# A pair's value product moved behind the next turn's scores, and scale totals moved to another PSUM bank, in attention followed by two gated MLPs

## The chip, the cores and the metric

The kernel runs on one core of a Trainium2 chip. The metric is device time in microseconds (us) from start to end of the program, as a median over runs. TensorE multiplies matrices into PSUM, ScalarE (ACT) and VectorE (DVE) read PSUM and compute element by element, GpSimd (POOL) does little here, and SyncE (SP) issues nearly all DMAs from one queue, in order.

## The reference

```python
def _attn_ref(q, k, v, g_q, g_k):          # 4 batches, 12 heads, 448 rows, 64 columns
    q_n, k_n = (rmsnorm(q, g_q), rmsnorm(k, g_k))
    scores = scale * np.matmul(q_n, k_n.transpose(0, 1, 3, 2))
    scores = scores - np.max(scores, axis=-1, keepdims=True)
    attn = np.exp(scores)
    attn = attn / (np.sum(attn, axis=-1, keepdims=True) + 1e-09)
    return np.matmul(attn, v)

def _moe_ref(x, w_a, w_b, w_out):          # x: 1792 x 768, hidden 1536
    return (x @ w_a) * (x @ w_b) @ w_out

def _moe2_ref(x, w_in, w_out, alpha):      # hidden 2048
    h = x @ w_in
    g = np.maximum(h, 0.0) + alpha * np.minimum(h, 0.0)
    return g @ w_out
```

The attention's output, all heads side by side, is the input of the first MLP, whose output is the input of the second. The weights come as 64-bit floats.

## The kernel before, in words

**Products.** Each of the four batches goes through four stages: `a` (24 products, w_a and w_b alternating, multiplied into `ab`), `y` (6), `h` (16) and `o` (6). They are named a0, y0, h0, o0, a1 and so on, and run in the order of the list `stages`. A number is held as two halves of 16 bits, so a product takes three matmuls for each block of 128 x 128: 18 matmuls for a product of `a` and `h`, 36 for one of `y`, 48 for one of `o`. A product accumulates in one of three PSUM banks (tiles `p`, pool `ps_m`). It is read out by L779 (ACT) and L782 (DVE) in `a`, L820 (ACT) in `y`, L857 and L858 in `h`, L876 (ACT) in `o`.

**Scales.** Halves of 16 bits need a scale by a power of two. For a stage's results it comes from the sum of their squares: L785 (in `a`, ACT) or L821 (in `y`) squares, a matmul with ones adds up over the partitions, VectorE makes the power, and then L760 (ACT) and L761 (DVE) split the results. So at the end of a stage all its results must be there before the next stage that uses them can start. Weights are converted on their first use, in a0, y0, h0 and o0 (L644, L647, L650, L658, then L705 and L706 behind a total over their squares), and kept in DRAM for the later batches, from where they are loaded four products ahead. All totals over squares go through `total` (tile `tot`), whose bank `x` (pool `ps_x`, one buffer) also serves the value products (tile `x`) and the norm of `y` (tile `norm`).

**Attention.** Heads go in pairs, six to a batch, 24 in all. `att_steps` is a generator. Its turn `m` issues the scores of step m + 1 (two chunks of 64 rows for two heads; seven chunks make a pair, so a pair takes three and a half turns), the softmax of step m (`soft`: maximum L417 on DVE, L430 and two exponentials L434 on ACT), the probabilities of step m - 1 (`probs`: L479 on ACT and L480 on DVE write one of four buffers `p16`, which a transposing DMA, L486, brings into `pT`), some preparation of later pairs (squares L232, L235, casts L341, L343), and, when a pair's chunks are all there, its value product `pv` (24 matmuls; 8 in batch 0, which uses 32-bit numbers) and `pv_out` (L530 on ACT, L531 on DVE), which reads it out of bank `x`. `pT` has one buffer: the next pair's transposes wait until the value product has read it. A turn has three yields.

**What runs when.** Ahead of a0 the loop `while done < NP` runs whole turns until the six pairs of batch 0 are done. From there each stage draws as many yields as the table `RATE` gives it, spread over its products, so that batches 1 to 3 are computed between products up to y2; a3 and the later stages have no attention. A scheduler then orders each engine's instructions, by the order in which they were written and by when it thinks that they can run; what it has made is fixed in the program.

Of the kernel before, what the change touches and what calls it, by code (L numbers as in the profile page):

```python
# [19 lines left out]
def attention_gated_mlps_kernel(  # L20
# [20 lines left out]
    NP = H // 2  # L41
# [79 lines left out]

    def total(cols, n, groups=1):

        ps = ps_x.tile([128, 512], F32, tag="x", name="tot")
        p = cols.shape[0]
        mm(ps[:, 0:n], ones[:p], cols, True, True)
        if n == groups:
            return ps[:, 0:n]
        t = sm_p.tile([128, 4], F32, tag="tot", name="tots")[:, 0:groups]
        nc.vector.reduce_sum(  # L130
            out=t, in_=ps[:, 0:n].rearrange("p (g k) -> p g k", g=groups), axis=AX.X
        )
        return t
# [406 lines left out]
    def att_steps():  # L540
        total = B * NP * NI // 2
        done = 0
        scores(0)
        for m in range(total + 3):
            if m + 1 < total:
                scores(m + 1)
            if m < total:
                soft(m)
            yield None
            if 1 <= m <= total:  # L550
                for _ in probs(m - 1):
                    yield None
            else:
                yield None
            fin = None
            for n in range(2 * m + 2 if m else 0, 2 * m + 4):
                g, c = divmod(n, NI)
                if n < 2 * total:
                    if g >= NP:
                        if c == 0 and g % NP == 0:  # L560
                            vscale(g // NP)
                        if c == 5:
                            vprep2(g)
                        if c == 6:
                            load_v(g + 2)
                    ahead = (g + 1, g + 2) if g % 2 else ()
                    if g > 1 and g % 2 == 0 and c == 6:
                        prep0(g + 2)
                    if c == 0:
                        for x in ahead[1 if g > 1 else 0:]:  # L570
                            prep0(x)
                    if c == 1 and ahead and g + 1 < B * NP:
                        prep1(ahead)
                    if g == 0 and c < NP:
                        vnorm(0, c)
                    if g == 1 and c == 0:
                        vscale(0)
                    if g == 0 and c < 3:
                        (prep3f, prep2f, prep4f)[c](1)
                    if 0 < g and g + 1 < B * NP and 2 <= c < 5:  # L580
                        (preps_f if g + 1 < NP else preps)[c - 2](g + 1)
                    if c == 5:
                        load_qk(g + 3)
                    if c == (6 if g % 2 or g < NP else 1) and g + NP < B * NP:
                        vnorm(g // NP + 1, g % NP)
            if done < B * NP and 2 * (m - 1) >= (done + 1) * NI:
                pv(done)
                pv_out(done)
                fin = done
                done += 1  # L590
            yield fin


    stages = "a0 y0 h0 o0 a1 y1 a2 h1 o1 y2 a3 h2 y3 o2 h3 o3".split()
# [323 lines left out]
    if True:  # L918
# [18 lines left out]
        n, done = 0, 0  # L937
        W0, EVERY = 4, 2
        while done < NP:
            g = [next(att) for _ in range(3)][-1]  # L940
            n += 1
            if n >= W0 and (n - W0) % EVERY == 0:
                advance((n - W0) // EVERY - 9 if n < 22 else -1)
            if n == 8:
                setup3()
                setup4()
            if g is not None:
                done += 1
# [51 lines left out]
```

## Time and profile before

| | |
|---|---|
| median of 3 runs | 1235.76 us (1233.34 to 1237.47) |
| profiled execution | 1237.6 us, span 1235.8 us |
| TensorE busy in the span | 1169.1 us (95%), 6574 matmuls |
| ScalarE busy | 738.8 us (60%) |
| VectorE busy | 677.4 us (55%) |
| mean granted TensorE clock | 0.981 |

The span is the time from the first to the last instruction. Busy shares are means over stages that differ: ScalarE and VectorE are busy nearly all the time early on, when weights are converted, and mostly idle at the end. Matmuls overlap, so that a busy TensorE isn't one at its peak; the time from one matmul's start to the next one's tells more. 1.0 of the granted clock is 2.4 GHz.

### The profile page before, as it was taken

How to read it: one execution, taken by the hardware profiler on the slowest of the kernel's cores; microseconds unless marked ns; L12 is line 12 of the kernel's file. 1: busy time of each engine (PE TensorE's matmuls, PEld its weight loads, DVE VectorE, ACT ScalarE, POOL GpSimd, SP SyncE). 2: the span in 40 equal slices, each digit the busy share in tenths (PEclk: the TensorE clock that was granted, in tenths of full speed). 3: DMA queues.
4: the chain of work that ended last, by engine and by line, in shares of the span. 5: the costliest groups of instructions: out<-in, count | busy, mean ns of one | idle time of the engine just before them, and what ended most of it. 6: DMA issues, size and time to landing. Idle time of an engine off the chain costs nothing.

```text
span 1235.8 us, 18195 instructions
## 1 busy us (share of the span) xinstructions
PE 1169.1 (95%) x6574; PEld 599.5 (49%) x6574; DVE 677.4 (55%) x1455; ACT 738.8 (60%) x1504; POOL 10.4 (1%) x32
## 2 busy tenths in 40 slices
PE   6997998989988999979999999999999999999998
PEld 4553554444534444435455454545555555554554
DVE  7898999889899667666551465331111440102400
ACT  7998999999889767676643465553221441213311
POOL 1000000000000000000000000000000000000000
PEclk9997999999999999989999999999999999999999
DMA  7558999999999999897854737876333333344343
GB/s 196 162 169 214 306 338 323 298 299 304 287 262 287 238 253 240 190 225 166 219 145 125 167 104 170 191 189 158 102 116 116 115 117 107 110 144 129 98 128 89
DMA packets 311243, 234.68 MB, mean 190 GB/s; under 512 B 175440, under 2 KB 284496, under 8 KB 311152
## 3 DMA queue, kind: packets, MB, share of 16 engines
q1 hardware_dynamic: 311040, 233.43, 71.7%
q8 instruction: 52, 0.85, 0.3%
q0 software_dynamic: 112, 0.07, 0.2%
q14 instruction: 39, 0.32, 0.1%
HBM read 155.79 MB, written 32.24 MB: 152 GB/s over the span
## 4 chain that ended last, share of the span: by engine, by line
PE 54%; DMA 2%; ACT 1%; DVE 1%; issue 0%; SPq 0%; ACTq 0%; DVEq 0%
PE p L107 49%; PE s L107 2%; PE x L107 2%; DMA pT<-p 2%; PE p L883 1%; ACT t L876 0%; PE norm L107 0%; ACT p L479 0%; ACT pf L434 0%; DVE nm L417 0%; SPq L486 0%; DVE ab L782 0%; DVE p L480 0%; DVE kr L332 0%; DVE qr L326 0%
## 5 line engine op out<-in xcount | busy, mean ns | idle before, releaser
L107 PEld LDWEIGHTS <-w 128*128 128x128 f16 x4896 | 476.7, 99 | 477.0 <-issue 49.7
L107 PE MATMUL p<-x,w 128*128 128x448 f16 x1728 | 336.8, 354 | 2.1 <-ACT t L779 2.0
L107 PE MATMUL p<-g,w 128*128 128x448 f16 x1152 | 229.5, 356 | 5.5 <-DVE g L844 2.1
L107 PE MATMUL p<-y,w 128*128 128x448 f16 x1152 | 224.7, 356 | 3.5 <-ACT y L760 3.2
L107 PE MATMUL p<-ab,w 128*128 128x448 f16 x864 | 170.8, 358 | 1.3 <-ACT ab L760 1.3
L417 DVE TENSOR_REDUCE nm<-s 128x2 f32<-128x896 f32 x84 | 91.1, 1085 | 41.7 <-PE s L107 41.3
L480 DVE SCALAR_TENSOR_TENSOR p<-pf,ri,p 128x448 f16<-128x448 f32 x126 | 84.4, 680 | 34.3 <-ACT p L479 34.0
L479 ACT ACTIVATE p<-pf,ri 128x448 f16<-128x448 f32 x126 | 81.4, 663 | 36.0 <-DMA pT<-p 28.1
L434 ACT ACTIVATE pf<-s,nm,esc 128x448 f32<-128x448 f32 x126 | 90.1, 719 | 1.3
L858 DVE SCALAR_TENSOR_TENSOR t<-t,al,p 128x448 f32<-128x448 f32 x55 | 37.3, 678 | 96.5 <-ACT t L857 96.5
L782 DVE SCALAR_TENSOR_TENSOR ab<-p,inv_a,t 128x448 f32<-128x448 f32 x48 | 32.5, 677 | 96.0 <-PE p L107 95.9
L706 DVE SCALAR_TENSOR_TENSOR w<-wf,sc,w 128x768 f16<-128x768 f32 (+1 forms) x76 | 70.2, 926 | 4.5 <-ACT w L705 4.1
L876 ACT ACTIVATE t<-p,inv_o 128x448 f32<-128x448 f32 x24 | 25.6, 1067 | 76.4 <-PE p L107 76.4
L785 ACT ACTIVATE junk<-ab 128x448 bf16<-128x448 f32 x48 | 27.4, 572 | 68.0 <-DVE ab L782 68.0
L650 DVE SCALAR_TENSOR_TENSOR wf<-raw,wf 128x768 int32<-128x768 int32 (+1 forms) x76 | 65.8, 867 | 0.5
L705 ACT ACTIVATE w<-wf,sc 128x768 f16<-128x768 f32 (+1 forms) x76 | 65.5, 866 | 0.0
L644 ACT ACTIVATE wf<-raw 128x768 f32<-128x768 f32 (+1 forms) x76 | 63.3, 838 | 1.6 <-DVE w L706 1.2
L658 ACT ACTIVATE junk<-wf 128x768 bf16<-128x768 f32 (+1 forms) x76 | 58.9, 775 | 2.9 <-DVE wf L650 2.5
L857 ACT ACTIVATE t<-p 128x448 f32<-128x448 f32 x55 | 29.7, 541 | 48.4 <-PE p L107 48.2
L843 ACT ACTIVATE g<-t,cgf 128x448 f16<-128x448 f32 x55 | 36.7, 668 | 34.6 <-DVE t L858 34.6
L107 PE MATMUL s<-kT,qT 128*64 128x448 f16 x252 | 50.2, 376 | 6.1 <-ACT pf L434 2.8
L844 DVE SCALAR_TENSOR_TENSOR g<-t,cgf,g 128x448 f16<-128x448 f32 x55 | 37.5, 682 | 29.6 <-ACT g L843 29.5
(140 smaller groups left out, 1065.1 us busy)
## 6 DMA issues: line engine op xcount, KB each, us to landing
w<-sc_a SPq DMA_DIRECT2D x72, 384.0 KB, 3.2
w<-sc_h SPq DMA_DIRECT2D x48, 384.0 KB, 3.0
w<-sc_o SPq DMA_DIRECT2D x72, 256.0 KB, 3.1
w<-sc_y SPq DMA_DIRECT2D x36, 384.0 KB, 3.2
raw<-in_moe_w_in_dram SPq DMA_DIRECT2D x16, 768.0 KB, 7.8
raw<-in_moe_w_out_dram SPq DMA_DIRECT2D x24, 512.0 KB, 5.9
raw<-in_moe_w_a_dram SPq DMA_DIRECT2D x12, 768.0 KB, 7.4
raw<-in_moe_w_b_dram SPq DMA_DIRECT2D x12, 768.0 KB, 7.5
```

What stands on the lines that cost most here:

```text
L107: nc.tensor.matmul(out=o, lhsT=a, rhs=b, start=first, stop=last)
L417: nc.vector.tensor_reduce(out=nm, in_=ps[:, :, 0:S], axis=AX.X, op=ALU.max, negate=True)
L434: nc.scalar.activation(out=pf, in_=ps[:, j, 0:S], func=AF.Exp, bias=nm[:, j:j + 1], scale=scale[j], accum_out=su[:, j:j + 1],)
L479: nc.scalar.activation(out=t[:, 0, :, 0:KP], in_=pf, func=AF.Copy, scale=r)
L480: nc.vector.scalar_tensor_tensor(out=t[:, 1, :, 0:KP], in0=pf, scalar=r, in1=t[:, 0, :, 0:KP], op0=ALU.mult, op1=ALU.subtract,)
L644: nc.scalar.activation(out=t, in_=hi.bitcast(F32), func=AF.Prelu, scale=2.0 ** -112, alpha=-(2.0 ** 32))
L650: nc.vector.scalar_tensor_tensor(out=ti, in0=lo, scalar=29, in1=ti, op0=ALU.logical_shift_right, op1=ALU.bitwise_or)
L658: nc.scalar.activation(out=junk(768, size(kind)), in_=t, func=AF.Square, accum_out=sums[0][:, j:j + 1])
L705: nc.scalar.activation(out=w[:, 0], in_=t, func=AF.Copy, scale=s)
L706: nc.vector.scalar_tensor_tensor(out=w[:, 1], in0=t, scalar=s, in1=w[:, 0], op0=ALU.mult, op1=ALU.subtract)
L844: nc.vector.scalar_tensor_tensor(out=x[:, 1], in0=t, scalar=cgf[:, f:f + 1], in1=x[:, 0], op0=ALU.mult, op1=ALU.subtract,)
L858: nc.vector.scalar_tensor_tensor(out=t, in0=t, scalar=al[:, f:f + 1], in1=ps, op0=ALU.mult, op1=ALU.add)
```

## The change

Two things change. The value product and its read-out (`pv`, `pv_out`) stand no longer at the end of turn m but right behind the scores at the start of turn m + 1, ahead of that turn's softmax. And `total` takes its bank from `new_ps`, which gives one of the three banks of the products, and no longer the bank `x`. The number of the finished pair comes with a turn's first yield, no longer with its third, and the loop ahead of a0 looks there.

```diff
     def total(cols, n, groups=1):
 
-        ps = ps_x.tile([128, 512], F32, tag="x", name="tot")
+        ps = new_ps()
         p = cols.shape[0]
...
         scores(0)
-        for m in range(total + 3):
+        for m in range(total + 4):
             if m + 1 < total:
                 scores(m + 1)
+            fin = None
+            if done < B * NP and 2 * (m - 2) >= (done + 1) * NI:
+                pv(done)
+                pv_out(done)
+                fin = done
+                done += 1
             if m < total:
                 soft(m)
-            yield None
+            yield fin
...
-            fin = None
             for n in range(2 * m + 2 if m else 0, 2 * m + 4):
...
-            if done < B * NP and 2 * (m - 1) >= (done + 1) * NI:
-                pv(done)
-                pv_out(done)
-                fin = done
-                done += 1
-            yield fin
+            yield None
...
         while done < NP:
-            g = [next(att) for _ in range(3)][-1]
+            g = [next(att) for _ in range(3)][0]
```

The scheduler makes a new order of all engines from this. The first place is ScalarE's queue just ahead of the read-out of pair 5's value product (L530), without which a0 can't finish a product. Before, in the built order:

```order
L644 ACTIVATE wf<-raw 128x768
L430 ACTIVATE nm<-nm,esc 128x2
L705 ACTIVATE w_1557<-wf,sc 128x768
L434 ACTIVATE pf,su<-s,nm,esc 128x448 x2
L462 COPY pT<-p 112x4x128 x2
L430 ACTIVATE nm<-nm,esc 128x2
L479 ACTIVATE p_2_110<-pf,ri 128x4x112
L434 ACTIVATE pf,su<-s,nm,esc 128x448 x2
L479 ACTIVATE p_3_111<-pf,ri 128x4x112
L658 ACTIVATE junk,ss<-wf 128x768
L530 ACTIVATE x_5_1467<-x,sx 128x448
```

The same place of ScalarE's queue with the change:

```order
L462 COPY pT<-p 112x4x128
L434 ACTIVATE pf,su<-s,nm,esc 128x448 x2
L462 COPY pT<-p 112x4x128
L430 ACTIVATE nm<-nm,esc 128x2
L235 ACTIVATE sq<-qr 128x448
L434 ACTIVATE pf,su<-s,nm,esc 128x448 x2
L479 ACTIVATE p_2_110<-pf,ri 128x4x112
L479 ACTIVATE p_3_111<-pf,ri 128x4x112
L430 ACTIVATE nm<-nm,esc 128x2
L232 ACTIVATE sk<-kr 112x512
L434 ACTIVATE pf,su<-s,nm,esc 128x448 x2
L530 ACTIVATE x_5_1476<-x,sx 128x448
```

A third softmax of 16-bit pairs stands ahead of L530, and squares of a later pair (L235, L232). Counted from the start of the queue, L434 stands 48 times ahead of this L530 instead of 46, L232 11 times instead of 9, L235 9 instead of 8, L430 3 instead of 2, and L644 9 instead of 10; the other lines as often as before.

The second place is ScalarE's queue at the end of y0, from the last squares (L821) to the first split for h0 (L760). Before:

```order
L821 ACTIVATE sq_2_2649<-y_0_5_3295 128x448
L434 ACTIVATE pf,su<-s,nm,esc 128x448 x2
L644 ACTIVATE wf<-raw 128x768
L705 ACTIVATE w_3437<-wf,sc 128x768
L479 ACTIVATE p_2_110<-pf,ri 128x4x112
L479 ACTIVATE p_3_111<-pf,ri 128x4x112
L341 CAST q_3490<-qr 128x7x64
L343 CAST k_3492<-kr 112x8x64
L760 ACTIVATE y_0_3331<-y_0_0_2724,sy 128x448
```

ScalarE at the end of y0 with the change:

```order
L821 ACTIVATE sq_2_2679<-y_0_5_3335 128x448
L644 ACTIVATE wf<-raw 128x768
L430 ACTIVATE nm<-nm,esc 128x2
L705 ACTIVATE w_3477<-wf,sc 128x768
L434 ACTIVATE pf,su<-s,nm,esc 128x448 x2
L760 ACTIVATE y_0_3371<-y_0_0_2754,sy 128x448
```

Probabilities and casts no longer stand between the two.

The third place is ScalarE's queue at the end of a2, from the last L779 to the last squares (L785), which the stage's total waits for. Before:

```order
L779 ACTIVATE t<-p,inv_a 128x448
L530 ACTIVATE x_0_7850<-x 128x448
L385 ACTIVATE v_8311<-vr,sx 112x8x64
L479 ACTIVATE p_1_109<-pf,ri 128x4x112
L479 ACTIVATE p_2_110<-pf,ri 128x4x112
L479 ACTIVATE p_3_111<-pf,ri 128x4x112
L785 ACTIVATE junk,ssab<-ab_2_11_7874 128x448
```

ScalarE at the end of a2 with the change:

```order
L779 ACTIVATE t<-p,inv_a 128x448
L785 ACTIVATE junk,ssab<-ab_2_11_7900 128x448
L430 ACTIVATE nm<-nm,esc 128x2
L434 ACTIVATE pf,su<-s,nm,esc 128x448
L760 ACTIVATE ab_0_7933<-ab_2_0_7204,sab 128x448
```

The read-out of a value product and three probabilities have gone from between the two.

## Rows read from the trace of the kernel before

**Rows 1.** Stretches: length; busy us (instructions) of PE, PEld, DVE, ACT, POOL; clock, DMA share, GB/s.

```profile
0.00:115.50 115.50, 91.62 (x553) 53.53 (x554) 98.25 (x299) 103.19 (x230) 5.21 (x15) 0.95 0.65 180
115.50:218.60 103.10, 97.29 (x557) 50.71 (x556) 97.13 (x199) 99.61 (x200) 0.71 (x1) 0.99 1.09 316
218.60:279.10 60.50, 53.37 (x299) 27.05 (x299) 52.96 (x113) 58.01 (x111) 0.61 (x2) 0.96 1.09 298
279.10:342.80 63.70, 63.28 (x346) 32.04 (x346) 58.18 (x115) 57.32 (x117) 1.61 (x3) 0.96 1.06 293
```

**Rows 2.** The chain that ended last, in a2: start us, us, what.

```profile
632.67 0.88 PE s L107 x8
633.55 20.53 PE p L107 x108
...
690.10 2.41 PE x L107 x24
```

**Rows 3.** Timeline, end of a0: start us, us, instruction [idle before <-releaser].

```profile
204.84 2.46 PE L107 MATMUL x<-pT,v 112*64 112x448 f16 x24 [0.82 <-DVE tots L130]
...
212.38 0.38 PE L107 MATMUL tot<-ss,ones 128*128 128x2 f32 x2 [1.56 <-DVE x L531]
...
214.04 0.67 ACT L479 ACTIVATE p<-pf,ri 128x448 f16<-128x448 f32 x1 [1.31 <-DMA pT<-p]
...
214.37 0.67 DVE L782 SCALAR_TENSOR_TENSOR ab<-p,inv_a,t 128x448 f32<-128x448 f32 x1
...
216.24 0.39 PE L107 MATMUL tot<-ssab,ones 128*128 128x12 f32 x2 [1.84 <-ACT junk L785]
...
218.63 2.83 PE L107 MATMUL p<-ab,w 128*128 128x448 f16 x8 [1.29 <-ACT ab L760]
```

**Rows 4.** Timeline, end of y0.

```profile
272.28 0.57 ACT L821 ACTIVATE sq<-y 128x448 bf16<-128x448 f32 x1
...
277.40 0.55 ACT L341 CAST q<-qr 128x448 f16<-128x448 f32 x1
...
277.85 0.61 ACT L343 CAST k<-kr 112x512 f16<-112x512 f32 x1
...
279.09 1.28 PE L107 MATMUL p<-y,w 128*128 128x448 f16 x3 [3.23 <-ACT y L760]
```

**Rows 5.** Timeline, end of a1.

```profile
546.62 0.67 ACT L479 ACTIVATE p<-pf,ri 128x448 f16<-128x448 f32 x1 [0.46 <-DMA pT<-p]
...
549.36 0.39 PE L107 MATMUL tot<-ssab,ones 128*128 128x12 f32 x2 [2.43 <-ACT junk L785]
```

**Rows 6.** Timeline, end of a2.

```profile
695.80 0.67 ACT L479 ACTIVATE p<-pf,ri 128x448 f16<-128x448 f32 x1 [2.12 <-DMA pT<-p]
...
700.00 0.39 PE L107 MATMUL tot<-ssab,ones 128*128 128x12 f32 x2 [1.92 <-ACT junk L785]
```

**Rows 7.** ScalarE's groups, 85 to 123 us: xcount | busy us, mean ns | idle before.

```profile
L644 ACT ACTIVATE wf<-raw 128x768 f32<-128x768 f32 x4 | 3.8, 949 | 0.0
L434 ACT ACTIVATE pf<-s,nm,esc 128x448 f32<-128x448 f32 x4 | 2.8, 707 | 0.0
...
L232 ACT ACTIVATE sk<-kr 112x512 f32<-112x512 f32 x2 | 1.4, 690 | 0.0
...
L235 ACT ACTIVATE sq<-qr 128x448 f32<-128x448 f32 x2 | 1.3, 644 | 0.0
...
L430 ACT ACTIVATE nm<-nm,esc 128x2 f32<-128x2 f32 x3 | 0.9, 296 | 1.6 <-DVE nm L417 1.6
...
L434 ACT ACTIVATION_READ_ACCUMULATOR pf<-s,nm,esc 128x1 f32 x4 | 0.8, 192 | 0.0
```

**Rows 8.** Timeline, h0: its products 11 to 13, and the thirteenth's read-out on VectorE.

```profile
319.58 10.61 PE L107 MATMUL p<-y,w 128*128 128x448 f16 x54
...
337.21 0.67 DVE L858 SCALAR_TENSOR_TENSOR t<-t,al,p 128x448 f32<-128x448 f32 x1
```

**Rows 9.** Stretch behind the end of a1: length, PE busy us, clock, DMA share, GB/s.

```profile
550.00:560.00 10.00, 8.47 (x34) 0.66 0.77 177
```

## Prediction

> **What bounds the kernel now.** I read the stretches first, cut at the stage borders: [rows 1] gives each engine's busy time, and the third number from the end is TensorE's granted clock. Up to 115.5 us, while the attention of batch 0 runs alone, ScalarE is busy 103.2 of 115.5 us and TensorE 91.6: this part is ScalarE's. In a0 (115.5 to 218.6) TensorE has 97.3 of 103.1 and ScalarE 99.6; in y0 ScalarE has 58.0 of 60.5, and only in h0 does it drop to 57.3 of 63.7. So until about 340 us TensorE and ScalarE hold each other, and time that TensorE wins there is kept only as far as ScalarE is no later. The chain that ended last, [rows 2], shows the rest: in a2 it is an unbroken row of products, 108 matmuls in 20.53 us (0.190 us each, 3.4 us for a product of 18), eight scores in 0.88 us, 24 value matmuls in 2.41 us. There, time is TensorE's work plus the moments at which it stands.
>
> It stands mostly at stage borders, where one scale needs all of a stage's results. [rows 3] is the end of a0: the value product of pair 6 (24 matmuls) first waits 0.82 us for a total's read out of the bank `x`; the next total waits 1.56 us until VectorE has read that value product out of the same bank; ScalarE waits 1.31 us in L479 for a probability buffer that a transposing DMA still reads; the total over a0's squares comes at 216.24 and y0's first product only at 218.63. The value product ended at 204.84 + 2.46 = 207.3, a0's last product of 18 at about 210.7: 7.9 us to y0, of which two groups of scores fill 1.8. [rows 4] is the end of y0 (last squares 272.28, first product of h0 279.09 after 3.23 us of waiting for L760), [rows 5] the end of a1 (the total waits 2.43 us), [rows 6] that of a2 (1.92 us).
>
> **The change, part by part.** First what isn't in its words. The value product comes one turn of the attention loop later, and the loop ahead of a0 runs until pair 5's value product is out: it makes one turn more (24, not 23). From there to the end of y2 the attention stands one turn ahead of the products: pair 6's value product stands behind 342 matmuls of the products, not 414, although it is one step later in its turn.
>
> *One turn more ahead of a0: +2.3.* On ScalarE, in the built order, more work stands ahead of pair 5's result (L530): two exponentials, two squares of K, one of Q, one L430, and one weight conversion (L644) less. By [rows 7]: 2 x (0.707 + 0.192) = 1.80; 2 x 0.69 = 1.38; 0.64; 0.30; less 0.95: 3.2 us. a0 can't pass its 16th matmul without L530. TensorE does eight scores in that time that it then needn't do later: less 0.88 [rows 2]. Net 2.3. Bounds: 0, if ScalarE's idle moments in that stretch take it in (the row of L430 has 1.6 us of idle ahead of it), and 5.0, what one turn of the 23 takes (115.5/23).
>
> *The bank `x` without totals: -2.0.* The 0.82 and 1.56 us of [rows 3] can't occur again: value products and totals share nothing, and pair 6's value product now stands 90 matmuls (17 us) ahead of a0's end, not 18, so that its transposes have landed before L479 asks. Both waits and L479's make 3.7 us at most; 0 if ScalarE, 97% busy in a0, is late by itself. I take 2.0, over half, since L479's wait is idle time of ScalarE itself.
>
> *The end of y0: -1.0.* Between the last squares (L821) and the first L760 stood two exponentials, L644, a weight split, two L479 and two casts; now L644, L430, the split and two exponentials. That is 2 x 0.67 + 0.55 + 0.61 less 0.30: 2.2 us less [rows 3, 4, 7]. But what is gone from here is done elsewhere by a ScalarE at 96%; I keep 1.0 of 0 to 2.2.
>
> *Totals in the big products' banks: +1.0.* There are three such banks. Each total takes one, so the product behind it must take that of the product two before, not three before: its read-out must be done within one product, 3.4 us, where it had two. At a0's end the read-out (L782) starts at 214.37 and ends 4.3 us after its product; in h0 the thirteenth product ends at 319.58 + 10.61 = 330.2 and its read-out L858 at 337.9, 7.7 us later [rows 3, 8]. So in the second half of a0, with six totals, a product can wait up to 0.9 us more, in h0 up to 4.3. Below, 0: at those places it is VectorE and ScalarE that are late, and TensorE waiting a little earlier for them moves nothing. Above, 6 x 0.9 = 5.4 for a0 alone. Nearest is the lower: the first products of o0 wait for L843 and L844 anyway. 1.0.
>
> *The end of a1: -1.2.* L479 waits there for transposes that could only be issued when the value product was done (546.62, [rows 5]), and L785 and the total stand behind it. The value product now stands two products ahead of the end, not one: 3.4 us more room, but two more L479 (1.3 us) stand ahead of L785. At most the total's whole wait, 2.43, goes; at worst nothing. Half.
>
> *The end of a2: -1.9.* Three L479 stood between the last L779 and the last L785, the first of which waits 2.12 us for the value product's transposes [rows 6]. In the new order none does, and the value product stands 90 matmuls ahead. The total's 1.92 goes. Bounds -1.9 and 0 (the second group of scores now stands ahead of that total and needs exponentials).
>
> The moved value product itself costs nothing: the same 24 matmuls, 2.41 us, run right behind scores. What waits for it are the next pair's transposes on SP's queue and ScalarE's L530; the weight loads behind those transposes are for products four ahead (14 us), which covers a step. In batch 0 the step also issues the load of V for two pairs on, one DMA that moves with it and has several turns to land.
>
> Sum: 2.3 - 2.0 - 1.0 + 1.0 - 1.2 - 1.9 = **-2.8**. The profiled execution took 1237.6 us, 1235.8 of them span; that is 1.8 over the median of the three runs, 1235.76, on which I put the sum: **1233.0 us**.
>
> **Rivals.** (1) *All of the borders' time is kept.* If ScalarE has room enough (10% in h0, [rows 1]), the ends of a0, y0 and a1 give 3.7, 2.2 and 2.4, a2 1.9, and the banks cost nothing: 2.3 - 10.2 = -7.9, 1228. For it: the waits are real rows of TensorE. Against: two of three lie where ScalarE is over 95% busy. (2) *The totals in the product banks decide: slower.* If read-outs are as late as in [rows 8] when a total has taken a bank, a0 loses 5.4, nothing is won at a0 and y0, and the turn ahead of a0 costs its 2.3: 2.3 + 5.4 - 1.2 - 1.9 = +4.6, 1240.5. It decides from the point at which a product's read-out ends more than 3.4 us after it while the other engines aren't late themselves. Against: in a0's first half the stretch is dense and its clock 0.99. (3) *Stalls that bring the clock down.* In the 10 us from 550, behind the wait at a1's end, the granted clock is 0.66 of 2.4 GHz [rows 9], that is 1.2 GHz for most of it, and costs 3.4 us; six stretches in a0 and h0 with half that loss would cost 10: 1243. The Trainium skill ("TensorE: Matmul & The Clock Gate", "A second HAM failure mode: psum-queue depth-cycling") says that cycling through PSUM banks makes TensorE pause so often between groups that its clock swings between half and full. The trace doesn't bear it out: a0 cycles three banks at 0.99. (4) *It does nothing*: the borders' waits take another form and the turn costs what they give; 1236.
>
> **Chances.** Forecast 0.44, (1) 0.24, (2) 0.15, (3) 0.04, (4) 0.13. A difference under 0.3% (3.7 us) can't be told from none: faster is below 1232.0, slower above 1239.5. The forecast's own range is 1229 to 1237, and about two fifths of it lie below 1232: faster 0.17 + 0.23 = 0.40. Slower: 0.14 of (2), all of (3) and a little of the rest, 0.19. Same: 0.41. The range for 8 in 10 leaves out (3) and the ends of (1) and (2): 1225 to 1241.
>
> **What would show it.** Right: a0's first product about 3 us later; no wait of a value product for `tots` nor of a total for L531; the first product of h0 under 5 us behind the last L821; the total at a2's end without a wait; from there on the same dense row, and one group of scores fewer behind a1. Wrong: products in a0 and h0 that wait for L779, L782 or L858 right behind a total (rival 2), a granted clock under 0.95 there (rival 3), waits of L479 for DMA above the 0.5 to 2.1 us of [rows 3, 5, 6], or a value product waiting for its own transposes.

## The result, and the profile after

The changed kernel takes 1242.92 us (median of 5 runs, 1242.38 to 1245.63), the kernel before in the same comparison 1235.31 (5 runs, 1233.09 to 1237.47): ratio 1.0067, 95% interval 1.0054 to 1.0080. It is slower, and the time lies above the predicted range of 1225 to 1241. Its profiled execution has a span of 1241.0 us, TensorE 1165.1 us busy, ScalarE 740.6, VectorE 677.5, mean granted clock 0.982: the same work as before, spread over more time.

The stretches, cut at the same stage borders as [rows 1] (columns as there):

```profile
0.00:119.50 119.50, 93.87 (x552) 53.56 (x553) 99.03 (x301) 104.12 (x231) 5.21 (x15) 0.93 0.65 187
119.50:224.80 105.30, 98.17 (x565) 51.27 (x563) 98.14 (x200) 103.52 (x208) 0.77 (x1) 0.99 1.04 300
224.80:281.80 57.00, 51.86 (x290) 26.48 (x290) 53.02 (x115) 55.35 (x107) 0.82 (x2) 0.95 1.10 305
281.80:354.10 72.30, 67.52 (x380) 34.81 (x379) 67.60 (x132) 66.50 (x134) 1.46 (x3) 0.96 1.09 297
```

a0 begins 4.0 us later and takes 2.2 longer, y0 is 3.5 shorter. (The last stretch isn't like for like: the value product that stood behind h0's end now stands ahead of o0.) To compare stages rightly, I cut the traces at products at which both kernels have done the same number of value matmuls, and since one execution may differ from the next, at three traces of each kernel (the two repeats are the runs r1 to r4 below). Length of each part in us, from one named product's start to the next; the columns end at a0's third product, y0's first, h0's first, a1's first, a2's thirteenth, a3's first, and the end. (Scores are not cut so evenly: with the change, "to a0" and "h0, o0" hold one group more, 0.9 us, and "y0" and "a2 to y2" one group less.)

| kernel | to a0 | a0 | y0 | h0, o0 | a1 to a2 | a2 to y2 | a3 on | span |
|---|---|---|---|---|---|---|---|---|
| before | 128.0 | 90.6 | 60.5 | 157.1 | 214.3 | 230.2 | 355.1 | 1235.8 |
| r1, before again | 128.8 | 90.5 | 59.4 | 158.0 | 212.4 | 228.4 | 355.1 | 1232.7 |
| r3, before, third | 128.5 | 91.5 | 60.0 | 156.7 | 213.7 | 228.3 | 355.2 | 1233.9 |
| after | 133.5 | 91.2 | 57.1 | 157.0 | 218.4 | 226.9 | 357.0 | 1241.0 |
| r2, after again | 132.5 | 92.6 | 56.1 | 155.6 | 218.1 | 226.8 | 357.0 | 1238.8 |
| r4, after, third | 135.0 | 92.2 | 56.4 | 155.4 | 221.0 | 226.9 | 357.0 | 1243.9 |
| difference of the means | +5.2 | +1.1 | -3.4 | -1.3 | +5.7 | -2.1 | +1.9 | +7.1 |

The columns scatter by up to 3 us within one kernel, the last one by 0.1. Three losses are larger than that: ahead of a0, in the part with a1, and in a3. y0 and the part with a2's end gain. The 7.1 us agree with the timed 8.3 (0.67% of 1235.31; interval 6.7 to 9.9).

**The end of a0.** Waits of TensorE from 182 us to y0, summed by who ended them: engine, tile, line, releaser: us in total, times, longest. Before:

```profile
PE tot L107 <- ACT junk L785: 1.8, 1, 1.8
PE tot L107 <- DVE x L531: 1.6, 1, 1.6
PE p L107 <- ACT ab L760: 1.3, 1, 1.3
PE x L107 <- DVE tots L130: 0.8, 1, 0.8
PE tot L107 <- DVE tots L130: 0.3, 1, 0.3
```

The same view of the changed kernel:

```profile
PE p L107 <- ACT junk L785: 3.1, 1, 3.1
PE p L107 <- ACT ab L760: 2.9, 1, 2.9
PE p L107 <- ACT t L779: 1.1, 2, 0.6
```

The two waits for bank `x` of [rows 3] (L531 and L130) are gone, as predicted. Those for ScalarE (L785, then L760) have grown from 3.1 to 6.0, and L779 adds 1.1 behind two totals: 7.1 in place of 5.8 (8.3 and 7.9 in the repeats, where before has 5.8 and 6.7). The waits had been standing in ScalarE's shadow.

**The end of y0**, which answers to [rows 4] (timeline; last squares, then h0's first product):

```profile
277.43 0.56 ACT L821 ACTIVATE sq<-y 128x448 bf16<-128x448 f32 x1
...
281.81 0.90 PE L107 MATMUL p<-y,w 128*128 128x448 f16 x2 [3.42 <-ACT y L760]
```

From the last L821 to h0 it is 4.4 us in all three traces, before 6.8, 6.3 and 7.0: about 2.4 won where 1.0 was predicted.

**h0**, the matmuls right behind three of its totals, which answers to [rows 8]:

```profile
316.15 3.56 PE L107 MATMUL p<-y,w 128*128 128x448 f16 x18 [0.52 <-DVE g L858]
...
325.37 10.38 PE L107 MATMUL p<-y,w 128*128 128x448 f16 x54 [1.15 <-DVE g L858]
...
341.08 3.56 PE L107 MATMUL p<-y,w 128*128 128x448 f16 x18 [0.83 <-DVE t L858]
```

Here the lost bank shows: the product behind a total waits for an older product's read-out, 2.5 us in three places. (In the repeats of before, one product of h0 waits 0.9 and 1.0 us for L858 too.) But the time isn't lost: o0's first products waited 3.1 to 3.6 us for L843 and L844 in the three traces of before and don't wait for them in any of the three with the change, and h0 with o0 is no longer than before.

**The end of a2**, which answers to [rows 6]:

```profile
703.56 0.35 PE L107 MATMUL s<-kT,qT 128*64 128x448 f16 x1
704.02 0.39 PE L107 MATMUL p<-ssab,ones 128*128 128x12 f32 x2
704.26 3.94 PE L107 MATMUL p<-y,w 128*128 128x448 f16 x20
```

The total has no wait (1.92, 1.82 and 1.73 in the three traces of before), and h1 follows without a gap: -1.9 predicted. From a2's thirteenth product to o1's first it is 107.4 us in all three traces, 109.3 and 109.4 in the repeats of before: -2.0. (The first trace of before has 111.1; only there did the granted clock fall in h1 behind the wait, to 0.97.) The -2.1 of the whole column agrees by chance: it also holds 1.5 us more in o1 and 1.0 less in y2, which has one group of scores less.

**a1**, which holds most of the loss. Waits of TensorE from a1's first product to y1's; before (436.2 to 553.2 us):

```profile
PE tot L107 <- ACT junk L785: 2.4, 1, 2.4
PE p L107 <- ACT t L779: 2.0, 1, 2.0
PE s L107 <- ACT pf L434: 1.8, 1, 1.8
```

and after (438.8 to 562.2 us):

```profile
PE p L107 <- DMA w<-sc_a: 3.6, 1, 3.6
PE p L107 <- ACT junk L785: 3.6, 1, 3.6
PE p L107 <- ACT t L779: 2.5, 1, 2.5
PE x L107 <- DVE ri L473: 1.7, 1, 1.7
```

6.2 us of waits have become 11.4. (The repeats: 7.1 and 6.9 before, 10.8 and 13.6 after, with much the same names.) The wait at a1's end of [rows 5] has not shrunk (2.43, 3.87 and 2.88 us before, 3.60, 2.86 and 3.89 after). Behind it now stands a value product that waits for its own probabilities: the view names L473, but the last of the transposes landed at 557.94 and the value product began at 558.03. Two waits in the middle stand at other places than before. This is TensorE at the first of them, at a1's products 11 and 12 (from 483.27), 13 and 14:

```profile
480.90 2.44 PE L107 MATMUL x<-pT,v 112*64 112x448 f16 x24
483.27 6.98 PE L107 MATMUL p<-x,w 128*128 128x448 f16 x36
...
491.06 3.58 PE L107 MATMUL p<-x,w 128*128 128x448 f16 x18
497.17 3.56 PE L107 MATMUL p<-x,w 128*128 128x448 f16 x18 [2.52 <-ACT t L779]
```

The product at 497.17 needs the bank of the one three before, whose 18 matmuls began at 483.27 and were over 3.5 us later. ScalarE reads it out only at 496.49:

```profile
493.35 0.54 ACT L530 ACTIVATE x<-x 128x448 f16<-128x448 f32 x1
493.77 0.72 ACT L385 ACTIVATE v<-vr,sx 112x512 f16<-112x512 f32 x1
494.38 0.56 ACT L341 CAST q<-qr 128x448 f16<-128x448 f32 x1
494.84 0.63 ACT L343 CAST k<-kr 112x512 f16<-112x512 f32 x1
495.36 1.23 ACT L479 ACTIVATE p<-pf,ri 128x448 f16<-128x448 f32 x2
496.49 0.63 ACT L779 ACTIVATE t<-p,inv_a 128x448 f32<-128x448 f32 x1
```

Read-out of the value product, casts of V, Q and K and two probabilities: 3.1 us, all ahead of L779. Before, ScalarE's queue at the same product had L779 first:

```profile
490.71 0.63 ACT L779 ACTIVATE t<-p,inv_a 128x448 f32<-128x448 f32 x1
491.23 0.55 ACT L530 ACTIVATE x<-x 128x448 f16<-128x448 f32 x1
491.65 0.73 ACT L385 ACTIVATE v<-vr,sx 112x512 f16<-112x512 f32 x1
```

That isn't all of it. L779 came 8.1 us after its product before and 9.7 us now, and before nothing waited for it, since the value product stood behind product 11 and gave TensorE 2.4 us of work until product 14 (at 492.79); now it stands ahead of product 11. TensorE before, products 12 to 14:

```profile
482.59 2.46 PE L107 MATMUL x<-pT,v 112*64 112x448 f16 x24
484.98 3.58 PE L107 MATMUL p<-x,w 128*128 128x448 f16 x18
...
489.37 6.98 PE L107 MATMUL p<-x,w 128*128 128x448 f16 x36
```

So the wait of 2.52 us is made by both orders together, the later read-out (1.6 us) and the earlier value product (2.4), less the 1.4 us by which L779 had been in time. Over the whole stage, counted from a product's start plus 3.5 us to its read-out's start, the read-outs of products 3 to 16 come 1.7 to 4.4 us later than before (means of three traces), and those of 17 to 23, behind the wait for `w<-sc_a`, 0.8 to 3.7 us earlier.

The Trainium skill ("Perfetto Trace Analysis", "Tensor Engine Instruction (MATMUL, LD_WEIGHTS)") says that ScalarE and VectorE take their instructions strictly first in, first out; the rows agree: L779's operand had been ready for 9.7 us, and it ran behind what stood ahead of it.

**a3's total.** Before, and after (timeline of TensorE):

```profile
962.78 1.68 PE L107 MATMUL p<-y,w 128*128 128x448 f16 x8
964.49 0.39 PE L107 MATMUL tot<-ssab,ones 128*128 128x12 f32 x2
```

```profile
967.85 0.39 PE L107 MATMUL p<-ssab,ones 128*128 128x12 f32 x2 [1.55 <-ACT junk L785]
968.10 1.11 PE L107 MATMUL p<-y,w 128*128 128x448 f16 x5
```

In bank `x` the total stood behind eight matmuls of h2's first product, which covered the squares that it waits for. In a bank of the products it stands ahead of them, and nothing covers the 1.55 us. All three traces of after have this wait, to 0.01 us.

### The profile page after: what moved, and what is told of

Read it like the earlier page. It is cut to its first block, busy times and chain, and to the rows that moved or that the text cites. A ratio compares the mean times of both kernels' runs of the same rounds, so it can differ in the third digit from the quotient of the medians.

```text
span 1241.0 us, 18166 instructions
## 1 busy us (share of the span) xinstructions
PE 1165.1 (94%) x6574; PEld 602.4 (49%) x6574; DVE 677.5 (55%) x1455; ACT 740.6 (60%) x1504; POOL 10.6 (1%) x32
## 5 line engine op out<-in xcount | busy, mean ns | idle before, releaser
L107 PE MATMUL p<-g,w 128*128 128x448 f16 x1152 | 226.1, 354 | 0.0
L417 DVE TENSOR_REDUCE nm<-s 128x2 f32<-128x896 f32 x84 | 91.2, 1086 | 44.8 <-PE s L107 44.4
L479 ACT ACTIVATE p<-pf,ri 128x448 f16<-128x448 f32 x126 | 81.7, 663 | 41.0 <-DMA pT<-p 33.9
L434 ACT ACTIVATE pf<-s,nm,esc 128x448 f32<-128x448 f32 x126 | 90.0, 718 | 1.3
L858 DVE SCALAR_TENSOR_TENSOR t<-t,al,p 128x448 f32<-128x448 f32 x55 | 37.3, 679 | 96.6 <-ACT t L857 96.5
L782 DVE SCALAR_TENSOR_TENSOR ab<-p,inv_a,t 128x448 f32<-128x448 f32 x48 | 32.5, 678 | 94.5 <-PE p L107 94.4
L785 ACT ACTIVATE junk<-ab 128x448 bf16<-128x448 f32 x48 | 27.4, 571 | 72.6 <-DVE ab L782 72.4
L705 ACT ACTIVATE w<-wf,sc 128x768 f16<-128x768 f32 (+1 forms) x76 | 64.4, 856 | 0.5 <-DVE sc L117 0.4
L644 ACT ACTIVATE wf<-raw 128x768 f32<-128x768 f32 (+1 forms) x76 | 62.1, 827 | 3.6 <-DMA raw<-in_moe_w_out_dram 2.1
L658 ACT ACTIVATE junk<-wf 128x768 bf16<-128x768 f32 (+1 forms) x76 | 58.4, 769 | 1.2 <-DVE wf L650 1.0
L843 ACT ACTIVATE g<-t,cgf 128x448 f16<-128x448 f32 x55 | 36.6, 666 | 34.0 <-DVE t L858 34.0
L844 DVE SCALAR_TENSOR_TENSOR g<-t,cgf,g 128x448 f16<-128x448 f32 x55 | 37.6, 683 | 31.9 <-ACT g L843 31.7
```

The lines of the kernel that those rows point to most:

```text
L107: nc.tensor.matmul(out=o, lhsT=a, rhs=b, start=first, stop=last)
L417: nc.vector.tensor_reduce(out=nm, in_=ps[:, :, 0:S], axis=AX.X, op=ALU.max, negate=True)
L434: nc.scalar.activation(out=pf, in_=ps[:, j, 0:S], func=AF.Exp, bias=nm[:, j:j + 1], scale=scale[j], accum_out=su[:, j:j + 1],)
L479: nc.scalar.activation(out=t[:, 0, :, 0:KP], in_=pf, func=AF.Copy, scale=r)
L644: nc.scalar.activation(out=t, in_=hi.bitcast(F32), func=AF.Prelu, scale=2.0 ** -112, alpha=-(2.0 ** 32))
L658: nc.scalar.activation(out=junk(768, size(kind)), in_=t, func=AF.Square, accum_out=sums[0][:, j:j + 1])
```

## The experiments

The change has three parts: the value product's place ("value"), the extra turn ahead of a0 ("turn"), the totals' bank ("bank"). Times are ratios to the kernel before in the same comparison, with 95% intervals. The same parts of the span as above, one trace each:

| run | parts | ratio | to a0 | a0 | y0 | h0, o0 | a1 to a2 | a2 to y2 | a3 on |
|---|---|---|---|---|---|---|---|---|---|
| before, mean of 3 | none | 1 | 128.4 | 90.9 | 60.0 | 157.3 | 213.5 | 229.0 | 355.1 |
| after, mean of 3 | all | 1.0067 | 133.7 | 92.0 | 56.5 | 156.0 | 219.2 | 226.9 | 357.0 |
| e1 | bank | 1.0035 | 125.4 | 93.8 | 63.1 | 153.7 | 215.6 | 230.1 | 356.5 |
| e2 | value, turn | 1.0077 | 130.3 | 93.8 | 57.6 | 157.7 | 224.2 | 226.1 | 355.0 |
| e3 | value, bank | 1.0161 | 134.1 | 88.4 | 61.0 | 155.1 | 224.8 | 231.8 | 357.0 |
| e4 | turn | 1.0083 | 129.9 | 96.5 | 59.1 | 155.0 | 219.1 | 227.6 | 355.1 |
| e5 | value | 1.0127 | 128.8 | 90.4 | 62.6 | 155.1 | 222.0 | 230.4 | 355.0 |
| e6 | all, six `p16` | 1.0057 | 135.6 | 93.1 | 57.6 | 159.4 | 213.2 | 226.0 | 356.5 |
| e7 | none, six `p16` | 1.0032 | 128.5 | 91.3 | 59.8 | 156.0 | 218.7 | 226.9 | 355.2 |
| e8 | all, batch 0 old | 1.0048 | 132.0 | 94.4 | 56.4 | 156.4 | 215.8 | 226.2 | 356.7 |
| e9 | bank but `ssab` | 1.0023 | 124.9 | 93.2 | 61.2 | 153.5 | 217.8 | 229.8 | 355.0 |
| e10 | value, turn, six `p16` | 1.0070 | 130.9 | 92.6 | 56.6 | 153.6 | 225.2 | 225.4 | 355.4 |
| e11 | as e8, `ssab` in `x` | 1.0043 | 129.6 | 95.7 | 57.3 | 160.4 | 216.4 | 226.1 | 355.2 |
| e12 | as e11, six `p16` | 1.0064 | 128.0 | 96.2 | 58.8 | 158.5 | 214.9 | 225.4 | 355.5 |
| e13 | all, loads earlier | 1.0069 | 133.7 | 91.8 | 56.7 | 156.5 | 219.8 | 226.2 | 356.9 |
| e14 | none, loads earlier | 0.9998 | 129.4 | 91.4 | 58.6 | 155.9 | 210.9 | 228.9 | 355.0 |

**e1, the bank alone** (against the kernel before):

```diff
-        ps = ps_x.tile([128, 512], F32, tag="x", name="tot")
+        ps = new_ps()
```

> The kernel before with one edit: a total takes a bank of the products. Value product and number of turns ahead of a0 stay. Theory A (the banks carry the loss): products in a0 and h0 wait about 0.5 to 1.2 us for a read-out right behind a total, as in the changed kernel, the total at the end of a3 waits about 1.5 us as there, and the ratio to before is 1.004 to 1.006. Theory B (the extra turn ahead of a0 carries it): only a3's 1.5 us shows, ratio 1.000 to 1.002. The prediction's own term was +1.0 us, 1.001.

1.0035 [1.0016, 1.0054]: between the theories. The last column shows a3's total (+1.4); a0, y0 and the part with a1 lose 8 in sum against the mean of before, "to a0" and h0 with o0 win 6.6. The bank is a cost of its own, but not all of it.

**e2, value and turn, totals in bank `x`** (the changed kernel with e1's lines the other way round):

> The changed kernel with the totals back in bank x: the value product is moved, the loop ahead of a0 has its 24th turn. Theory A (banks): the loss goes, 0.998 to 1.001 of before; a3's total has no wait. Theory B (the turn): a0's first product stays about 4 us late and 1.003 to 1.005 is left. In both the waits of totals for a value product's read-out at the end of a0 (0.82 and 1.56 us before) may come back, since both use bank x again, if the value product stands near a total.

1.0077 [1.0054, 1.0099]: as slow as the whole change, so theory A fails as the main cause. a3 is as before to 0.1 us, which ties its 1.9 us to the bank. But the loss isn't at a0's start either (+1.9): it is in the part with a1, 224.2 against 213.5.

**e3, value and bank without the turn.** Pair 5 at its old place, the loop as long as before:

```diff
-            yield None
+            fin = None
+            if done == NP - 1 and 2 * (m - 1) >= (done + 1) * NI:
+                pv(done)
+                pv_out(done)
+                fin = done
+                done += 1
+            yield fin
...
-            g = [next(att) for _ in range(3)][0]
+            g = [next(att) for _ in range(3)]
+            g = g[0] if g[2] is None else g[2]
```

> The changed kernel, but pair 5's value product stays at the end of turn 22, so that the loop ahead of a0 makes 23 turns as before; all other value products are moved, totals in the products' banks. Theory B (the turn): a0's first product comes at 115.5 us within 1 us, and the loss shrinks to 1.000 to 1.003 of before. Theory A (banks): 1.005 to 1.007 stays. A third theory, that the moved value products delay weight loads in a1 (3.6 us of waiting for a load in the changed kernel), expects that wait to stay wherever the attention stands at that place.

1.0161 [1.0135, 1.0186], and a0's third product at 134.1: theory B expected the opposite. Without the turn the later parts (224.8, 231.8) lose more than with it (219.2, 226.9); which wait makes that wasn't looked for.

**e4, the turn alone** (against the kernel before, behind the loop ahead of a0):

```diff
+        for _ in range(3):
+            next(att)
         state["pin"] = False
```

> The kernel before with three more yields of the attention drawn ahead of a0, nothing else. Theory B: a0's first product 3 to 5 us later, of which one group of scores (0.9 us) comes back: ratio 1.002 to 1.004. The prediction's term was +2.3 us, bounds 0 and 5.0. Theory A: 0.999 to 1.002, since no total changes its bank.

1.0083 [1.0063, 1.0104], twice what theory B gave. Ahead of a0 it costs 1.5 us, near its term (2.3); but a0 then loses 5.6 and the part with a1 5.6. The turn is not over when a0 has begun, which the prediction had assumed.

**e5, value alone** (e3 with totals in `x`):

> The value products moved, all but pair 5's, which stays at the end of turn 22: no turn more ahead of a0, totals in bank x. It completes a table of the three parts of the change (value, turn, bank). If the parts add, it is value and turn (1.0077) less turn alone (1.0083): 0.999. If the moved value product costs by itself where the attention isn't a turn ahead, as the run of the changed kernel without the turn (1.0161) suggests, 1.008 to 1.015, and the time goes in a1, by ScalarE's waits in L479 for the transposes (4.2 us before, 7.9 to 12.8 in the runs with moved value products).

1.0127 [1.0106, 1.0149]: the parts don't add (0.999 expected if they did). The part with a1 is 222.0, +8.5, as expected; but L479's waits for transposes in a1 are 6.0 us, not the 7.9 to 12.8 that were to carry it.

**e6, e7, e10: six buffers of probabilities**, in the changed kernel, in before, and in e2:

```diff
-    p16 = [acts.tile([128, 2, KB, 128], F16, name=f"p16_{i}") for i in range(4)]
+    p16 = [acts.tile([128, 2, KB, 128], F16, name=f"p16_{i}") for i in range(6)]
```

> The changed kernel with six buffers of probabilities (p16) in place of four. Theory C (the next pair's transposes come later behind the moved value product, L479 waits for its buffer, and ScalarE's read-outs of products stand behind it): those waits in a1 fall from 7.9 us to below 3, a1 takes 118 to 120 us from its first product to y1's (123.4 in the changed kernel, 117.0 before), ratio to before 1.001 to 1.004. Theory D (it is the weight load behind the transposes on SyncE's queue that is late, 3.6 us): a1 stays over 121 us, ratio 1.005 to 1.008.

> The control: the kernel before with six buffers of probabilities. If L479's waits in the kernel before (4.2 us in a1, 5.2 in y1, 3.7 in a2) cost TensorE time as the prediction took it for the ends of a1 and a2, ratio 0.996 to 0.999; if they are idle time of ScalarE only, 0.999 to 1.001.

> Value products moved, turn added, totals in bank x, six buffers of probabilities. Theory C: the 12.6 us that a1 loses against before with four buffers (129.6 us from its first product to y1's, 117.0 before) shrink to below 4, ratio 1.000 to 1.004 (1.0077 with four). If the buffers had nothing to do with it, 1.006 to 1.009.

e6: 1.0057 [1.0034, 1.0080], e7: 1.0032 [1.0018, 1.0047], e10: 1.0070 [1.0048, 1.0092]. In e6 the part with a1 is back at 213.2 (118.7 us from a1's first product to y1's), as theory C said, though the ratio stays above C's range: other parts took the gain. But e10 has the same buffers and keeps its 225.2, with no more such waits (7.0 us) than the changed kernel (6.1 to 7.9 us in three traces, and 218.1 to 221.0). So theory C falls as the whole account. The row of L479 in a1, first of e2 and then of e10 (us busy, mean ns, idle before and who ended it):

```profile
L479 ACT ACTIVATE p<-pf,ri 128x448 f16<-128x448 f32 x30 | 19.5, 664 | 15.6 <-DMA pT<-p 12.8 <-ACT pf L434 1.0 <-DVE ri L473 0.9
```

```profile
L479 ACT ACTIVATE p<-pf,ri 128x448 f16<-128x448 f32 x28 | 18.2, 663 | 8.7 <-DMA pT<-p 7.0 <-ACT pf L434 1.5
```

The waits for transposes nearly halve and TensorE gains nothing: its waits in a1 are 15.0 us in e2 and 15.3 in e10, under other names (L779 6.2 and 4.0; in e10 also 3.0 for the DMA of `qS` and 2.9 for the value product's own transposes). e7 shows the size of such effects: more buffers alone made before slower by 0.3%, which neither expectation held, and the part with a1 longer by 5.2.

**e8, the changed kernel with pairs 0 to 4 at the old place:**

```diff
-            if done < B * NP and 2 * (m - 2) >= (done + 1) * NI:
+            if NP - 1 <= done < B * NP and 2 * (m - 2) >= (done + 1) * NI:
...
-            yield None
+            fin = None
+            if done < NP - 1 and 2 * (m - 1) >= (done + 1) * NI:
+                pv(done)
+                pv_out(done)
+                fin = done
+                done += 1
+            yield fin
...
+            g = [next(att) for _ in range(3)]
+            g = g[0] if g[2] is None else g[2]
```

> The changed kernel, but pairs 0 to 4 have their value products at the old place; pair 5 and all later ones are moved, the 24th turn and the totals' banks stay. If a0's delay (5.5 us at its third product) comes from batch 0's moved value products, whose results come 5 to 7 us later in pairs 1 to 3, it is 1.5 to 3 us here, as with the turn alone (1.8); the later stages are as in the changed kernel, so 1.003 to 1.005. If the delay comes from pair 5's own place and the totals, 5 to 6 us stay and 1.006 to 1.008.

1.0048 [1.0031, 1.0065], the ratio that the first theory gave, but with a0's third product at 132.0, 4.0 us after that of the first trace of before, where it gave 1.5 to 3. e11's queues of TensorE and ScalarE are in the same order up to a0's end, and it has 129.6. So 2.4 us of such a difference are one execution's, and the head can't be taken apart further from single traces.

**e9, e11, e12: the stages' totals back in `x`**, the other totals in the products' banks; against before, in e8, and in e8 with six buffers:

```diff
-    def total(cols, n, groups=1):
+    def total(cols, n, groups=1, x=False):
...
+        ps = ps_x.tile([128, 512], F32, tag="x", name="tot") if x else new_ps()
...
-        power(total(ssab[:, b % 2], KF), sab[:, b:b + 1], iab[:, b:b + 1])
+        power(total(ssab[:, b % 2], KF, x=True), sab[:, b:b + 1], iab[:, b:b + 1])
```

> The kernel before with only the totals over weights, V and Q, K in the products' banks; the totals over the stages' results (ssab) stay in bank x. With all totals moved the ratio was 1.0035, and the total at the end of a3 came 1.9 us later by its place behind more of h2's matmuls. Theory E (that total is a lasting part of the cost of the banks): h2's first product stands within 0.5 us of a3's offset, ratio about 1.002. Theory F (all of the cost lies in a0 and h0, where products wait behind totals of weights): 1.003 to 1.004 stays.

> The changed kernel with pairs 0 to 4 at the old place and the stages' totals in bank x. Against the same with all totals in the products' banks (1.0048), a3's 1.9 us should go: 1.002 to 1.004 by theory E, and 1.004 to 1.006 if it comes back elsewhere.

> The same with six buffers of probabilities, put together from what each run gained: a1's waits of L479 halved, a3's total without its wait, batch 0 nearly as before. If parts add, 0.998 to 1.001 of before; if each new order of the queues ahead of a0 sets its own time, anything from 0.998 to 1.006, with the difference made by a0's third product already.

e9: 1.0023 [1.0006, 1.0039], e11: 1.0043 [1.0026, 1.0059], e12: 1.0064 [1.0043, 1.0086]. In all three a3 is within 0.4 us of before; theory E holds for that term. It isn't all that there is: e9 still loses in the part with a1, and e12, put together from what each run had gained, isn't faster than its parts (its 1.0064 lies just above both of its ranges).

**r1 to r4: both kernels again, without an edit, for two more traces each.**

> The kernel before, unchanged, profiled once more. If one execution's trace is the kernel's, each stage starts within 0.5 us of the first trace, a0's third product at 128.0. If executions scatter as the timed runs do (1230 to 1239 us), stages move by up to 3 us, and the place where they do tells which of the differences between before and after can be read from one trace: the head, where DMA and four engines hold each other, more than the dense rows of a2.

> The changed kernel, unchanged, profiled once more. Theory C: a1 takes over 121 us again and L479 waits 6 us or more in it for transposes; the total at a3's end waits 1.5 us again. The head: a0's third product at 133.5 within 0.5 us if the 5.5 us belong to the change; 130 to 133 if part of it was one execution's.

> As the second profile of before. If the first trace was a slow one (its execution took 1237.6 us, the medians of 17 to 19 runs lie at 1233.5 to 1234.7), this one ends 2 to 5 us earlier, and the place where it does is the same as in the second.

> As the second profile of the changed kernel: a1 over 121 us, a3's total with its wait of 1.5 us, the wait at a0's first border over 5 us in sum (7.1 in the first trace, 5.8 before); the weight load that a1 waited 3.6 us for may land in time here if it was one execution's delay.

They give the first table. Before's first trace is 1.9 to 3.2 us longer than the two others, mostly in the parts with a1 and a2; after's first lies between its two others. The head's loss is 3.7 to 7.0 between any two traces, a1's 3.8 to 8.6, a3's 1.8 to 1.9; the wait for `w<-sc_a` came each time (3.6, 3.3, 3.7 us).

**e13, e14: weights loaded one product earlier**, in the changed kernel and in before:

```diff
-    wh_p = ctx.enter_context(tc.tile_pool(name="wh", bufs=5))
+    wh_p = ctx.enter_context(tc.tile_pool(name="wh", bufs=6))
...
-    AGAIN = [(w_load, 4)]
+    AGAIN = [(w_load, 5)]
```

> The changed kernel with weights loaded five products ahead in place of four, and six weight buffers in place of five. Theory D (the load that comes late behind transposes on SyncE's queue sets a1's time): a1's wait for w<-sc_a goes, and from a1's first product to a2's thirteenth it takes 214.5 to 216.5 us (218.1 to 221.0 in three traces of the changed kernel, 212.4 to 214.3 before); ratio 1.003 to 1.005. Theory G (ScalarE's and VectorE's read-outs are as late, and the wait only changes its name): 218 to 221 us stay, ratio 1.005 to 1.008.

> The control: the kernel before with the same two edits. It has no wait for a weight load in a1, so nothing is to be won there: 212 to 215 us from a1's first product to a2's thirteenth, ratio 0.998 to 1.001. If the order of the queues alone costs something, as six probability buffers did (1.0032), 1.002 to 1.004.

e13: 1.0069 [1.0050, 1.0089], e14: 0.9998 [0.9980, 1.0017]. TensorE's waits in e13's a1:

```profile
PE p L107 <- ACT junk L785: 4.1, 1, 4.1
PE p L107 <- ACT t L779: 3.0, 1, 3.0
PE x L107 <- DVE ri L473: 2.0, 1, 2.0
PE p L107 <- DVE ab L782: 1.1, 1, 1.1
```

The load's 3.6 us are gone and the part takes 219.8, no less than before the edit: L782, L785 and L473 have become the waits. Theory G holds, as far as an edit can show it that makes a new order itself: TensorE is held in a1 by ScalarE's and VectorE's read-outs, and the late load stood in their place. e14 shows no difference that can be measured. No version here beats the kernel before.

## Why the prediction was wrong

**The step that failed: "The moved value product itself costs nothing", and with it the turn priced only ahead of a0.** I gave the part with a1 -1.2; it measured +5.7 (3.8 to 8.6 between any two traces). I had counted what waits for the value product (transposes, L530) and found each covered. I had not asked what the new order of ScalarE's queue puts ahead of the products' read-outs in a1, the stage with the densest attention. e4 (turn alone, +5.6), e5 (value alone, +8.5) and e2 (both, +10.7) show that the value product's place and the turn each lengthen that part, by more than the 1.9 to 2.9 us by which traces of one kernel differ. The rows of the changed kernel show how it happens at one place: L530, three casts and two L479 in front of an L779 whose product had long been done, and a value product that no longer fills TensorE's time until that bank is needed. ScalarE is busy only 79.75 of 117.0 us in before's a1 (the fourth of the five engines in the row), a share that the prediction, which called ScalarE late by itself only at 95% and above, took for room:

```profile
436.20:553.20 117.00, 110.70 (x662) 53.21 (x661) 81.34 (x177) 79.75 (x184) 0.19 (x1) 0.97 1.01 226
```

It is room only for a queue that may change its order. Two things stay open. What an edit that shortens just that stretch of the queue would give wasn't tried. And neither part of the change is needed for such a loss: e9, which moves only the banks of some totals, takes 120.6 us from a1's first product to y1's (116.0 to 116.9 in the three traces of before), e7 loses 5.2 in the whole part, and e14 wins 2.6. So how much of the 5.7 comes from the value product and the turn as such, and how much any new order would have cost against an order that happens to be a good one, isn't shown. The largest change in ScalarE's own waits there, L232's for a load of K (2.6 to 3.3 us before, 10.5 to 12.6 after), doesn't make the loss alone: e14 has 8.7 and the shortest a1.

**One turn more ahead of a0 (+2.3).** Alone it costs +1.5 there (e4), near the term, as far as one trace can tell. The whole change costs +5.2. Over the same stretch, up to a0's third product, ScalarE, before and after:

```profile
0.00:128.00 128.00, 104.12 (x622) 59.16 (x623) 108.56 (x319) 114.09 (x255) 5.21 (x15) 0.95 0.69 186
```

```profile
0.00:133.50 133.50, 107.87 (x630) 60.00 (x631) 110.48 (x325) 116.40 (x260) 5.21 (x15) 0.94 0.67 190
```

Its work grew by 2.3 us: the exponentials, squares and L430 that were counted and one more L235, less L644 and also one L658 and one L705, which weren't. Its idle time grew by 3.2 (13.9 to 17.1; 13.9 to 14.5 in the three traces of before, 16.3 to 18.9 after). This second half came with value and bank together (e3 has it without the turn), not with the bank alone, which lost 3 us of idle there. TensorE's busy time grew by 3.75 us in these rows, of which eight scores are 0.9, at a granted clock of 0.94 and not 0.95. Which of the many short waits make up the loss, and whether the clock is a part of it or follows from them, stays open.

**The bank `x` without totals (-2.0).** The waits named are gone, the gain isn't: 7.1 us of waits stand where 5.8 stood, a0 is 1.1 longer. The bound of 0 was the right end. Its own reason was in the text: ScalarE is late there by itself.

**The end of y0 (-1.0).** Right in place, too small: y0 is 3.4 shorter. 0.9 of it is a group of scores that the turn had already done; e2 (57.6, bank `x`) shows that it comes from value and turn together; the turn alone (59.1) gives that group, and value and bank alone give nothing (62.6, 63.1).

**Totals in the products' banks (+1.0).** Right in mechanism, too small, and one place was missed: a3's total costs 1.9, where I had looked at no stage without attention; e9 against e1 shows that share. In a0 the waits behind totals are 1.1. In h0 they are 2.5, but h0 with o0 isn't longer for it (-1.3; e1, the bank alone, -3.6), which fits the reason of the lower bound, that o0's first products wait for L843 and L844 anyway. Timed alone the bank costs 0.35%, 4.3 us.

**The end of a1 (-1.2).** Nothing won: 2.43, 3.87 and 2.88 us in three traces of before, 3.60, 2.86 and 3.89 after, with the value product's own wait of 1.0 to 1.7 behind it. That last wait stood in the prediction as a sign that it would be wrong.

**The end of a2 (-1.9).** Right: no wait, and 2.0 less than in the repeats of before up to o1.

**The rivals.** Rival 2 gave 1240.5; its sign, products that wait right behind a total, came with 1.1 us in a0, where it had put 5.4. The time is nearest to rival 3's 1243, by luck: neither is what happened, and the banks alone are 1.0035. Rival 3 has a small share: behind the 3.61 us wait for the load the clock of the next 5 us is 0.71, which makes that product take 4.93 us and not 3.58:

```profile
513.10:518.00 4.90, 4.88 (x20) 2.06 (x19) 4.56 (x18) 3.70 (x11) 0.00 (x0) 0.71 0.75 188
```

Over the whole span the clock is no lower than before (0.981 to 0.983 in three traces, 0.981 to 0.984 before), and in a0, where totals now take banks too, it is 0.99 in both. So the rule of the Trainium skill ("TensorE: Matmul & The Clock Gate") that rival 3 names decides nothing here. What no rival held was that a dense stage in the middle could lose, where ScalarE is busy two thirds of the time and reads products out too late all the same.

## What to carry to other kernels

A stage in which an in-order engine is only two thirds busy can still be held up by it: look not at busy time but at how long each read-out comes after its product, and at how much work the matrix engine has until it needs that bank again (8.1 us late cost nothing here, 9.7 us with 2.4 us less of such work cost 2.5). Compare the built order of both queues before pricing a moved step at nothing. A shift of a generator by one turn is a change to every stage that draws from it, and the parts of such a change don't add: value, turn and bank alone cost 1.3, 0.8 and 0.4%, all three together 0.7%. A wait that is taken away at a border gives only what the next engine in line is not late by itself.

## What the runs showed that I had not expected

- Two executions of the same queue order differ by up to 3 us in the early stages (128.0 and 128.8, 132.5 and 135.0 at a0's third product; 218.1 and 221.0 in a1's part), while the stages from a3 on repeat to 0.1 us. A difference of that size in an early stage can't be read from one pair of traces.
- A wait of 2.98 us at the same place in a1 left the next product at full clock in r4 (18 matmuls in 3.57 us) and lowered it in e13 (5.17 us, granted clock 0.67 over those 4.9 us).
- Two more buffers of probabilities, which only take waits away, cost the kernel before 0.32% [0.18, 0.47]; the new order of the queues is the only reason at hand, and it wasn't taken apart.
